# Heads paired across two groups, with 64-row by 32-column TensorE tiles for the landmark scores

## The chip, the cores and the metric

The kernel runs on one core of a Trainium2 chip. The metric is the device time of one execution in microseconds (us); of several runs the median is taken. Engines are written as the profile writes them: PE is TensorE's matmuls, PEld its weight loads, DVE is VectorE, ACT is ScalarE, POOL is GpSimd, and SP issues the DMAs.

## The reference, cut to what matters

A Nyström attention over 8 batches, 8 heads, 576 tokens and a head size of 64, with 32 landmarks, is followed by a Fourier mixing over tokens and channels, a normalisation and a two-layer network of width 2048.

```python
q_lm = q.reshape(B, H, m, S // m, D).mean(axis=3)      # m = 32 landmarks of 18 tokens
k_lm = k.reshape(B, H, m, S // m, D).mean(axis=3)
A = sm(q, k_lm)          # softmax(scale * q @ k_lm^T): 576 x 32 per head
Bm = sm(q_lm, k_lm)      # 32 x 32 per head
C = sm(q_lm, k)          # 32 x 576 per head
Z = Bm^T / (|Bm|_1 * |Bm|_inf + 1e-6)
for _ in range(6):
    Z = 2 * Z - Z @ Bm @ Z
attn = A @ Z @ C @ v
x = attn, heads side by side           # 8 x 576 x 512
u = x + real(fft(fft(x, axis=1), axis=2))
un = (u - mean(u)) / sqrt(var(u) + 1e-6)
out = u + relu(un @ w_ch1) @ w_ch2
```

## The kernel before, in words

The inputs are laid out on the host. The eight heads of a batch stand in two groups of four (`GROUPS`), and each group in two pairs. q and k lie with the head size on the partitions: a pair's two heads take rows 0 to 63 and 64 to 127 of a 128-row tile. `load(b)` brings, for each group g, one tile `kf` of k (two pairs, 1152 columns) and one tile `qf` of q (1168 columns), each by one DMA of 128 rows, then v and, for batch 0, the first pieces of the weights. These tiles come from the pool `big`.

Work of a batch is written as two Python generators. `tokens(b)` sums tokens into landmarks on DVE (`lm`: columns 0 to 63 of a group are q's, 64 to 127 k's), bounds q with a sum of absolute values on ACT (`AF.Abs`, into `am`), scales and splits q and the k landmarks into two fp16 halves, and computes A: block u = 0 and u = 1 is a group each, four token tiles by two pairs by three matmuls of 64 columns; u = 2 holds the remaining 64 tokens of both groups (the rest, tile `row`). Then come softmax, the transposed copies `AT`, the sums and differences `F1`, `F2`, `Fh` over mirrored token tiles, and the cosine and sine products `CS`. `landmarks(b)` computes B and C in fp32. Because a pair shares the 128 rows, q's landmarks are first spread into `qbd`, 64 columns a pair, with the other head's rows set to zero by a mask; one matmul of a 128-row by 64-column tile then serves both heads. C goes in two column halves of 288 per group. B's softmax, the iteration for Z (`RE`, `E`), and the folded tables `Wt`, `Wx` and `WC` follow; `mix` puts it together per token tile, `norm` normalises and hands tiles `unT` to the network.

`mlp` is the network: a chunk of 256 tokens takes 192 matmuls `h<-unT,w` (256 columns) and 96 matmuls `acc<-w,h` (512 columns). `weights` decodes the 32 weight pieces from 64-bit words at the start (PE sums their squares into `acc<-w`; from these `scale` makes the scales `wsc`) and halves them into fp16 pairs. The network's second layer can begin only when the second scale, computed from all 32 pieces, is there.

PE's order is written by the program: `run` steps the threads attention, weights and mlp by a clock of its own (`now`), and each thread says with `till` how long it would wait. While nothing is ready and the first accumulator is not yet needed, it puts matmuls `acc<-idle` on PE. The other engines' orders come from a scheduler, except for instructions that `keep_in_program_order` fixes. Every engine runs its list in order. The PSUM banks `at` of the attention are four, used in turn (`psum`); a fifth request waits until the first is read.

All calls on DVE, ACT and POOL go through `Timed.emit`, so the profile shows them at L127; all matmuls show at L210, transposes on PE at L215. In the profile's names `w` is the weights, `at` a bank of the attention, `ones` a matrix of ones.

Of the kernel before, what the change touches and what calls it, by code (L numbers as in the profile page):

```python
# [41 lines left out]
OFF = 768  # L42

# [61 lines left out]
class Timed:  # L105


    def __init__(self, kernel, engine, fixed, rate, fast):
        self.kernel, self.engine, self.fixed, self.rate, self.fast, self.free = kernel, engine, fixed, rate, fast, 0.0

    def __getattr__(self, name):
        call = getattr(self.engine, name)

        def emit(out, *args, **kw):
# [12 lines left out]
            return call(out, *args, **kw)  # L127
# [4 lines left out]
class Kernel:  # L132
    def __init__(self, ctx, tc, NB, q, k, v, w1, w2, t1, t1t, t2, diag, mask, out):
# [9 lines left out]
        self.V, self.A = Timed(self, nc.vector, 0.07, 1.04e-3, 0.52e-3), Timed(self, nc.scalar, 0.2, 0.83e-3, 0.83e-3)  # L143
# [216 lines left out]
    def load(self, b):  # L360
# [4 lines left out]
        for g in range(2):  # L365
            kf, qf = self.big(), self.big()
            gs = slice(2 * g, 2 * g + 2)
            nc.sync.dma_start(kf[:, 0 : 2 * S].rearrange("p (r t) -> p r t", r=2), self.k[b, :, gs])
            nc.sync.dma_start(qf[:, 0 : 16 * SEG].rearrange("p (r t) -> p r t", r=2), self.q[b, :, gs])
# [12 lines left out]
    def tokens(self, b, st):  # L382
# [6 lines left out]
        lm = sm.tile([P, 2, 128], F32, name="lm", bufs=1)  # L389
        am = self.small(4, "amax")  # L390
        qbd = sm.tile([P, 4, 64], F32, name="qbd", bufs=1)
        qhs = []
        for g in range(2):
            kf, qf = loads[g][0][:, 0 : 2 * S], loads[g][1][:, 0:NQ]
            first = V.tensor_reduce(lm[:, g, 64:128], kf.rearrange("p (m t) -> p m t", t=18), AX.X, ALU.add)
# [3 lines left out]
            lv = lm[:, g, 0:64].rearrange("p (x o m) -> p x o m", o=2, m=8)  # L399
# [6 lines left out]
            A.activation(qhs[g][:, 0:NQ], qf, AF.Abs, accum_out=am[:, g : g + 1])  # L406
# [18 lines left out]
        klm = sm.tile([P, 2, 2, 64], F16, name="klm", bufs=1)
        kbd = sm.tile([P, 2, 2, 2, 64], F16, name="kbd", bufs=1)
        for g in range(2):
            split(klm[:, g, 0], klm[:, g, 1], lm[:, g, 64:128], sc[:, g : g + 1])
        for h2 in range(2):
            ms, cols = self.mask2[:, h2 : h2 + 1], slice(32 * h2, 32 * h2 + 32)  # L430
            V.tensor_scalar(
                kbd[..., cols].rearrange("p g y r m -> p (g y r) m"), klm.rearrange("p g y (r m) -> p (g y r) m", r=2),
                ms, None, ALU.mult,
            )
        qm = [h[:, 0:2048].rearrange("p (y r t) -> p y r t", y=2, r=2) for h in qhs]
        qr = [h[:, 2048:2304].rearrange("p (y r t) -> p y r t", y=2, r=2) for h in qhs]
        for g in range(2):
# [6 lines left out]
            if g == 0:  # L444
                yield self.till(qhs[0], kbd)
# [90 lines left out]
    def landmarks(self, b, st):  # L536
# [39 lines left out]
        while b == 1 and self.seconds < NF // 2 - HB:  # L576
            yield 0.5
# [446 lines left out]
```

## Time and profile before

| | |
|---|---|
| median of 3 runs | 1018.75 us (1017.17 to 1018.84) |
| profiled execution | 1018.43 us, of which the profiled span is 1016.6 us |
| PE, busy share of the span | 969.0 us, 95% |
| PEld | 673.3 us, 66% |
| DVE | 608.2 us, 60% |
| ACT | 335.5 us, 33% |
| POOL | 125.9 us, 12% |
| mean granted TensorE clock | 0.98 |

How to read what follows. A row of the view by groups gives line, engine, operation, `out<-in` by the program's names, shapes and count; then busy time in us and the mean length of one in ns; then the engine's idle time before such instructions and what ended it. `128*64` is the part of the array that a matmul takes: 128 rows, 64 columns. An fp32 matmul of the program shows as two records. Matmuls are pipelined, so the length of a record is not its price; the price is the distance to the next start. A row of the timeline gives start, length, engine, operation and count, and in brackets the idle time before it with the releaser. A row of the table by stretches gives, after the stretch's bounds and length, the busy us of PE, PEld, DVE, ACT and POOL with their counts, the granted clock, the DMA share and GB/s.

### The profile page before, as it was taken

How to read it: one execution, taken by the hardware profiler on the slowest of the kernel's cores; microseconds unless marked ns; L12 is line 12 of the kernel's file. 1: busy time of each engine (PE TensorE's matmuls, PEld its weight loads, DVE VectorE, ACT ScalarE, POOL GpSimd, SP SyncE). 2: the span in 40 equal slices, each digit the busy share in tenths (PEclk: the TensorE clock that was granted, in tenths of full speed). 3: DMA queues.
4: the chain of work that ended last, by engine and by line, in shares of the span. 5: the costliest groups of instructions: out<-in, count | busy, mean ns of one | idle time of the engine just before them, and what ended most of it. 6: DMA issues, size and time to landing. Idle time of an engine off the chain costs nothing.

```text
span 1016.6 us, 20320 instructions
## 1 busy us (share of the span) xinstructions
PE 969.0 (95%) x8407; PEld 673.3 (66%) x8407; DVE 608.2 (60%) x1654; ACT 335.5 (33%) x723; POOL 125.9 (12%) x144
## 2 busy tenths in 40 slices
PE   5776989999999999999999999999999999999998
PEld 3654756667776676666766776667676676666665
DVE  6979797786655855287556855686453834351111
ACT  4658653343223322142233323332212322111110
POOL 0000000013011400024011401122020220110000
PEclk8887999999999999999999999999999999999999
DMA  9863204142312240112402240225020200120000
GB/s 328 254 250 111 83 2 167 22 71 51 148 21 45 43 164 11 43 36 53 161 12 53 50 168 6 58 48 180 1 53 11 58 15 22 22 53 21 1 22 21
DMA packets 97772, 74.63 MB, mean 73 GB/s; under 512 B 68112, under 2 KB 86544, under 8 KB 97552
## 3 DMA queue, kind: packets, MB, share of 16 engines
q1 hardware_dynamic: 97680, 73.34, 24.7%
q8 instruction: 66, 1.08, 0.5%
q14 instruction: 26, 0.21, 0.1%
HBM read 48.02 MB, written 9.44 MB: 57 GB/s over the span
## 4 chain that ended last, share of the span: by engine, by line
PE 82%; DVE 11%; ACT 3%; DMA 2%; issue 1%; POOL 1%; SPq 0%; DVEq 0%; POOLq 0%; ACTq 0%
PE h L210 34%; PE acc L210 34%; PE at L210 13%; DVE w L127 2%; DVE mid L127 1%; ACT mid L127 1%; DMA mid<-mid 1%; DVE lm L127 1%; DVE cmx L127 1%; DVE asum L127 1%; DMA big<-q_dram 1%; DMA big<-k_dram 1%; POOL mid L127 1%; PE at L215 1%; DVE amx L127 0%
## 5 line engine op out<-in xcount | busy, mean ns | idle before, releaser
L210 PE MATMUL h<-unT,w 128*128 128x256 f16 x3456 | 411.2, 273 | 0.0
L210 PEld LDWEIGHTS <-w 128*128 128x128 f16 (+1 forms) x3584 | 346.2, 99 | 73.2 <-issue 3.3
L210 PE MATMUL acc<-w,h 128*128 128x512 f16 x1680 | 394.3, 380 | 0.0
L210 PEld LDWEIGHTS <-h 128*128 128x128 f16 x1680 | 161.8, 98 | 161.9 <-issue 4.4
L127 DVE SCALAR_TENSOR_TENSOR h<-h 128x512 f16<-128x512 f32 x140 | 96.1, 687 | 198.7 <-ACT h L127 198.0
L127 ACT ACTIVATE h<-h 128x512 f16<-128x512 f32 x140 | 83.2, 595 | 308.0 <-PE h L210 295.8
L127 POOL TENSOR_TENSOR r<-ve,mhalf 128x2 f32<-128x2 f32 (+1 forms) x20 | 13.7, 685 | 411.1 <-DVE ve L127 404.1
L127 POOL TENSOR_TENSOR mid<-mid 128x640 f16<-128x640 f32 (+2 forms) x36 | 40.9, 1144 | 114.2 <-ACT mid L127 107.9
L127 DVE TENSOR_TENSOR mid<-mid 128x256 f32<-128x256 f32 (+2 forms) x68 | 45.3, 682 | 13.2 <-DMA mid<-mid 9.4
L127 DVE TENSOR_REDUCE lm<-big 128x32 f32<-128x576 f32 (+1 forms) x48 | 44.2, 946 | 10.2 <-DMA big<-k_dram 9.5
L127 DVE SCALAR_TENSOR_TENSOR u<-at,scw,row 128x128 f32<-128x128 f32 (+3 forms) x120 | 38.6, 389 | 13.8 <-PE at L210 11.8
L210 PEld LDWEIGHTS <-big 128*128 128x128 f16 (+1 forms) x768 | 39.7, 101 | 10.2 <-issue 2.8
L210 PEld LDWEIGHTS <-mid 64*128 64x128 f16 (+1 forms) x624 | 30.0, 96 | 18.8 <-issue 8.6
L127 ACT CAST row<-row 128x512 f16<-128x512 f32 (+1 forms) x40 | 20.7, 551 | 62.7 <-DVE row L127 62.7
L127 DVE SCALAR_TENSOR_TENSOR row<-at,scw,row 128x262 f32<-128x262 f32 (+1 forms) x48 | 21.3, 486 | 28.3 <-ACT row L127 21.4
L127 POOL TENSOR_TENSOR row<-row 128x512 f16<-128x512 f32 (+1 forms) x33 | 34.3, 1055 | 30.7 <-ACT row L127 28.8
L210 PE MATMUL at<-RE,E 128*128 128x96 f32 (+1 forms) x192 | 30.5, 281 | 4.3 <-DVE RE L127 4.3
L127 DVE SCALAR_TENSOR_TENSOR u<-acc,wsc,u 128x512 f32<-128x512 f32 x36 | 26.8, 749 | 12.5 <-PE acc L210 11.8
L210 PEld LDWEIGHTS at<-RE,E 128*128 128x128 f32 x192 | 27.1, 194 | 10.6 <-DVE RE L127 4.4
L210 PE MATMUL at<-mid,big 128*128 128x262 f16 (+1 forms) x288 | 31.8, 279 | 0.0
L127 DVE SCALAR_TENSOR_TENSOR big<-big,aq_r 128x1024 f16<-128x1024 f32 (+1 forms) x32 | 26.8, 868 | 3.9 <-ACT big L127 3.9
L127 ACT CAST mid<-mid 128x512 f16<-128x512 f32 (+1 forms) x28 | 18.1, 671 | 28.2 <-POOL mid L127 20.5
(166 smaller groups left out, 928.6 us busy)
## 6 DMA issues: line engine op xcount, KB each, us to landing
w<-w_dram SPq DMA_DIRECT2D x22, 512.0 KB, 8.7
big<-v_dram SPq DMA_DIRECT2D x16, 640.0 KB, 8.9
big<-q_dram SPq DMA_DIRECT2D x16, 584.0 KB, 6.0
big<-k_dram SPq DMA_DIRECT2D x16, 576.0 KB, 5.0
out_dram<-u SPq DMA_DIRECT2D x36, 256.0 KB, 2.0
big<-w_dram SPq DMA_DIRECT2D x10, 512.0 KB, 6.8
t<-t_dram SPq DMA_DIRECT2D x1, 1048.0 KB, 9.2
unT<-row SPq DMA_TRANSPOSE x64, 2.5
```

The lines of the kernel that those rows point to most:

```text
L127: return call(out, *args, **kw)
L210: self.nc.tensor.matmul(out, a, b, start=start, stop=stop, skip_group_check=True)
L215: self.nc.tensor.transpose(out, a, ident)
```

## The change

A 128-row tile now pairs a head of group 0 (rows 0 to 63) with a head of group 1 (rows 64 to 127); the loop variable e goes over the pairs within a group. Each tile of q and k is loaded by two DMAs of 64 rows.

- B and C need no `qbd`: a matmul takes 64 rows (one head) and 32 columns. A batch has 8 of them for B and 16 for C instead of 4 and 8. All four banks are asked for at once (`till(lm, banks=4)`); B's result lies in columns 288 to 319 of the first two. The two row halves write different banks.
- In A the `kbd` mask goes over the groups. Blocks u = 0 and 1 are now two token tiles each with all heads; the count of 64-column matmuls stays 48. The rest takes 24 matmuls of 32 columns instead of 12 of 64.
- One scale for q and one for k instead of one a group: `am` has two columns, `qsum` adds them, `km` is the maximum over both tiles; `scr` and its copies go. q's bound no longer waits for the landmarks.
- `F1` is formed from both A blocks, 512 columns an operation; `CS` and `mix` index accordingly.
- ACT's first ten instructions keep the program's order (`PIN`): q's two sums of absolute values come first.

```diff
+PIN = 10
...
+            ins = call(out, *args, **kw)
+            if self.pinned > 0:
+                self.kernel.tc.keep_in_program_order(ins)
+                self.pinned -= 1
+            return ins
...
-            nc.sync.dma_start(kf[:, 0 : 2 * S].rearrange("p (r t) -> p r t", r=2), self.k[b, :, gs])
-            nc.sync.dma_start(qf[:, 0 : 16 * SEG].rearrange("p (r t) -> p r t", r=2), self.q[b, :, gs])
+            for t, src, n in ((kf, self.k, S), (qf, self.q, 8 * SEG)):
+                for half in range(2):
+                    nc.sync.dma_start(
+                        t[64 * half : 64 * half + 64, 0 : 2 * n].rearrange("p (o t) -> p o t", o=2),
+                        src[b, :, 2 * half + g].rearrange("(o p) t -> p o t", o=2),
+                    )
...
-            for h2 in range(2):
-                ms, cols = self.mask2[:, h2 : h2 + 1], slice(32 * h2, 32 * h2 + 32)
-                V.tensor_scalar(
-                    qbd[:, 2 * g : 2 * g + 2, cols], lm[:, g, 0:64].rearrange("p (r m) -> p r m", r=2), ms, None, ALU.mult
-                )
-            yield self.till(qbd)
+            yield self.till(lm)
...
+        V.tensor_tensor(qs, am[:, 0:1], am[:, 1:2], ALU.add)
+        eq, rq = self.power(qs, 1, 2.0**-13, "aq", b == 1)
...
+            if u < 2:
+                pt = ps.rearrange("p (j g r m) -> p j g r m", j=2, g=2, r=4)
+                for j in range(2):
+                    for r in range(4):
+                        at = 128 * (2 * u + j)
+                        mm3(pt[:, j, :, r], lambda y: qm[r // 2][:, y, r % 2, at : at + 128], lambda y: kbd[:, y, r // 2, r % 2].rearrange("p (g m) -> p g m", g=2))
+            else:
+                for r in range(4):
+                    for g in range(2):
+                        mm3(ps[64 * g : 64 * g + 64, 32 * r : 32 * r + 32], lambda y: qr[r // 2][:, y, r % 2],
+                            lambda y: kbd[:, y, r // 2, r % 2, 32 * g : 32 * g + 32])
...
-        ps = self.psum()
-        for g in range(2):
-            for pr in range(2):
-                mm(ps[64 * pr : 64 * pr + 64, 32 * g : 32 * g + 32], qbd[:, 2 * g + pr], lm[:, g, 64 + 32 * pr : 96 + 32 * pr])
-        V.tensor_scalar(Bd.rearrange("p g m -> p (g m)"), ps[:, 0:64], 1.0 / 2592.0, None, ALU.mult)
+        while b == 1 and self.seconds < NF // 2 - HB:
+            yield 0.5
+        yield self.till(lm, banks=4)
+        heads = [(slice(64 * g, 64 * g + 64), slice(32 * r, 32 * r + 32), g, r // 2, r % 2) for r in range(4) for g in range(2)]
+        halves = [[self.psum() for g in range(2)] for hf in range(2)]
+        for half, row, g, e, o in heads:
+            mm(halves[0][g][row, 288:320], lm[half, 0, e, 32 * o : 32 * o + 32], lm[half, 1, e, 32 * o : 32 * o + 32], share=0.3)
+        for hf in range(2):
+            for half, row, g, e, o in heads:
+                kv = loads[e][0][half, S * o + 288 * hf : S * o + 288 * hf + 288]
+                mm(halves[hf][g][row, 0:288], lm[half, 0, e, 32 * o : 32 * o + 32], kv, share=0.21)
```

Three places show how the lists of the engines move. The first is ACT at the program's start; `big,amax<-big` are q's sums of absolute values, `mid,csum<-at,cb` C's exponentials, `row<-w` and `w<-w` the decoding of weights. Before:

```order
L127 ACT_TABLE_LOAD
L127 ACTIVATE row<-w_74 128x512
L127 ACTIVATE Bd<-Bd 128x64
L127 ACTIVATE row<-w_74 128x512
L127 ACTIVATE w_73<-w_74 128x512
L127 ACTIVATE mid,csum<-at,cb 128x288 x3
L127 ACTIVATE big,amax<-big 128x1168 x2
L127 ACTIVATE mid,csum<-at,cb 128x288
```

And now:

```order
L130 ACT_TABLE_LOAD
L130 ACTIVATE big,amax<-big 128x1168 x2
L130 ACTIVATE row<-w_74 128x512
L130 ACTIVATE Bd<-Bd 128x64
L130 ACTIVATE mid,csum<-at,cb 128x288 x4
L130 ACTIVATE row<-w_74 128x512
L130 ACTIVATE w_73<-w_74 128x512
L130 ACTIVATE klm<-lm,sc 128x128
```

The two sums stand ahead of everything else and no longer behind three exponentials; weight decoding moves back.

The second is DVE ahead of batch 0's first normalised tile (`unT`), on which the network's first matmul waits; `w_73<-w_73,wsc` halves a piece of the first layer. Before:

```order
L127 SCALAR_TENSOR_TENSOR r_992<-rt,r_990 128x2
L127 SCALAR_TENSOR_TENSOR w_73<-w_73,wsc 128x512
L127 TENSOR_SCALAR row<-u,mv,r_992 128x512 x2
L127 SCALAR_TENSOR_TENSOR w_73<-w_73,wsc 128x512
L127 SCALAR_TENSOR_TENSOR w_74<-row,w_74 128x512
L127 SCALAR_TENSOR_TENSOR w_73<-w_73,wsc 128x512
L127 SCALAR_TENSOR_TENSOR unT<-at,unT 128x4x128 x2
```

And now:

```order
L130 SCALAR_TENSOR_TENSOR r_986<-rt,r_984 128x2
L130 SCALAR_TENSOR_TENSOR w_73<-w_73,wsc 128x512
L130 TENSOR_SCALAR row<-u,mv,r_986 128x512 x2
L130 SCALAR_TENSOR_TENSOR w_73<-w_73,wsc 128x512
L130 SCALAR_TENSOR_TENSOR w_74<-row,w_74 128x512 x2
L130 SCALAR_TENSOR_TENSOR unT<-at,unT 128x4x128
```

Over the whole list, 10 halvings and 23 decodings stood ahead of the first `unT`; now 3 and 20 do.

The third is DVE between the second scale (`wsc`) and the landmarks of batch 1, which PE waits for; `big<-big,aq_r` splits q, `lm<-big` are the landmark sums. Before:

```order
L127 TENSOR_SCALAR wsc<-wp_e 128x1
L127 SCALAR_TENSOR_TENSOR w_74<-w_74,wsc 128x512
L127 SCALAR_TENSOR_TENSOR h<-h 128x512
L127 SCALAR_TENSOR_TENSOR w_74<-w_74,wsc 128x512 x3
L127 SCALAR_TENSOR_TENSOR h<-h 128x512
L127 SCALAR_TENSOR_TENSOR w_74<-w_74,wsc 128x512 x4
L127 TENSOR_REDUCE lm<-big 128x64
```

And now:

```order
L130 TENSOR_SCALAR wsc<-wp_e 128x1
L130 SCALAR_TENSOR_TENSOR big<-big,aq_r 128x1024
L130 SCALAR_TENSOR_TENSOR h<-h 128x512
L130 SCALAR_TENSOR_TENSOR w_74<-w_74,wsc 128x512
L130 SCALAR_TENSOR_TENSOR big<-big,aq_r 128x128
L130 SCALAR_TENSOR_TENSOR w_74<-w_74,wsc 128x512
L130 SCALAR_TENSOR_TENSOR big<-big,aq_r 128x1024
```

The four operations that split q moved ahead of the landmark sums; before, they stood behind C.

More of the change, by code (lines that the diff above doesn't have):

```diff
@@ L388, in tokens @@
         NQ = 16 * SEG
-        lm = sm.tile([P, 2, 128], F32, name="lm", bufs=1)
-        am = self.small(4, "amax")
-        qbd = sm.tile([P, 4, 64], F32, name="qbd", bufs=1)
+        lm = sm.tile([P, 2, 2, 64], F32, name="lm", bufs=1)
+        am = self.small(2, "amax")
         qhs = []
-        for g in range(2):
-            kf, qf = loads[g][0][:, 0 : 2 * S], loads[g][1][:, 0:NQ]
-            first = V.tensor_reduce(lm[:, g, 64:128], kf.rearrange("p (m t) -> p m t", t=18), AX.X, ALU.add)
+        for e in range(2):
+            kf, qf = loads[e][0][:, 0 : 2 * S], loads[e][1][:, 0:NQ]
+            first = V.tensor_reduce(lm[:, 1, e], kf.rearrange("p (m t) -> p m t", t=18), AX.X, ALU.add)
             if b == 1:
                 self.tc.keep_in_program_order(first)
-            lv = lm[:, g, 0:64].rearrange("p (x o m) -> p x o m", o=2, m=8)
+            lv = lm[:, 0, e].rearrange("p (x o m) -> p x o m", o=2, m=8)
             qv = qf.rearrange("p (x o t) -> p x o t", o=2, t=2 * SEG)
@@ L414, in tokens @@
-        st["loads"], st["qbd"], st["lm"] = loads, qbd, lm
+            A.activation(qhs[e][:, 0:NQ], qf, AF.Abs, accum_out=am[:, e : e + 1])
+            yield self.till(lm)
+        kb = self.small(2, "kb", BF16)
+        km, qs = self.small(1, "kmax"), self.small(1, "qsum")
+        V.tensor_reduce(km, lm[:, 1].rearrange("p e m -> p (e m)"), AX.X, ALU.max, apply_absolute_value=True)
+        st["loads"], st["lm"] = loads, lm
         self.spawn(self.landmarks(b, st))
-        eq, rq = self.power(am[:, 0:2], 2, 2.0**-13, "aq", b == 1)
@@ L425, in tokens @@
+        sc = self.small(2, "sc")
+        V.tensor_tensor(sc[:, 0:1], eq, rk, ALU.mult)
+        V.tensor_scalar(sc[:, 1:2], ek, 1.0 / 144.0, None, ALU.mult)
         klm = sm.tile([P, 2, 2, 64], F16, name="klm", bufs=1)
         kbd = sm.tile([P, 2, 2, 2, 64], F16, name="kbd", bufs=1)
+        split(*(klm[:, y].rearrange("p e m -> p (e m)") for y in range(2)), lm[:, 1].rearrange("p e m -> p (e m)"), sc[:, 0:1])
         for g in range(2):
-            split(klm[:, g, 0], klm[:, g, 1], lm[:, g, 64:128], sc[:, g : g + 1])
@@ L539, in landmarks @@
         V, A = self.V, self.A
-        loads, qbd, lm = st["loads"], st["qbd"], st["lm"]
+        loads, lm = st["loads"], st["lm"]
         m4g = lambda m: self.mask4.unsqueeze(1).unsqueeze(3).broadcast_to([P, 2, 4, m])
@@ L574, in landmarks @@
         V.tensor_tensor(BTd, wide(BT, 32), m4g(32), ALU.mult)
-        while b == 1 and self.seconds < NF // 2 - HB:
-            yield 0.5
         for g in range(2):
-            kv = loads[g][0][:, 0 : 2 * S].rearrange("p (r t) -> p r t", r=2)
             Ce = self.mid()
@@ L584, in landmarks @@
             csum, cmx = self.small(2, "csum"), self.small(2, "cmx")
[L585 removed]
             for hf in range(2):
[L587 to L591 removed]
+                V.tensor_reduce(cmx[:, hf : hf + 1], halves[hf][g][:, 0:288], AX.X, ALU.max)
             cb = self.small(1, "cb")
```

90 lines of the change are left out of this document (29 added, 61 removed).

## The prediction

> **What bounds the kernel.** I read the page first, then the table by stretches.
>
> ```profile
> PE 969.0 (95%) x8407; PEld 673.3 (66%) x8407; DVE 608.2 (60%) x1654; ACT 335.5 (33%) x723; POOL 125.9 (12%) x144
> ```
>
> ```profile
> 119.50:140.00 20.50, 16.40 (x90) 7.57 (x88) 19.79 (x56) 13.43 (x26) 0.00 (x0) 1.00 0.00 0
> 175.00:1016.00 841.00, 832.79 (x7106) 572.87 (x7104) 462.28 (x1253) 233.02 (x512) 117.94 (x127) 1.00 0.20 54
> ```
>
> From 175 us to the end PE is busy for 832.79 of 841 us at full clock, while DVE, ACT and POOL are idle about half the time or more. So there a microsecond of matmuls saved is a microsecond of the span, and work saved on the other engines is worth nothing. Between 119.5 and 140 us it is the reverse: DVE is busy for 19.79 of 20.5 us and PE waits. Before that come the loads, batch 0 and the decoding of the weights, a stage set by chains. I therefore make three sums: batches 2 to 7, batch 1, and the start.
>
> **Batches 2 to 7: B and C.** The timeline of PE in batch 2, and two places later and earlier where the array is shared by several small tiles:
>
> ```profile
> 218.50 0.43 PE L210 MATMUL at<-lm,qbd 128*64 128x32 f32 x8
> 218.76 2.14 PE L210 MATMUL at<-big,qbd 128*64 128x288 f32 x16
> 220.83 1.04 PE L210 MATMUL acc<-w,h 128*128 128x512 f16 x4
> ...
> 235.58 1.73 PE L210 MATMUL at<-big,mid 128*32 128x64 f32 x80
> 237.24 1.27 PE L210 MATMUL at<-kbd,big 128*128 128x64 f16 x36
> ...
> 189.69 0.84 PE L210 MATMUL at<-Wx,mid 64*128 64x128 f16 x24
> 190.46 2.14 PE L210 MATMUL h<-unT,w 128*128 128x256 f16 x18
> ```
>
> B and C take 220.83 - 218.50 = 2.33 us. C's 16 records run in pairs, one on each 64-column half: 2.07 / 8 = 0.259 us a pair. Afterwards C has 32 records on eight tiles (two row halves, four column strips). Eight at a time that is 4 x 0.259 = 1.04 us; B's 16 records are two rounds where four pairs took 0.26 us, so 0.13 us; together 1.17 us. If only four ran at a time, C would stay at 8 x 0.259 = 2.07 us and B at 0.26 us: no gain. No row shows rows and columns divided at once, but each division is shown alone. Four 32-column strips: 80 records in 1.66 us are 0.021 us each, where 64 columns at the pair's pace need 0.259 x 64/288 = 0.058 us. Two row halves: 24 records in 0.77 us are 0.032 us each, where half of an `h` record (below, 0.109 us) is 0.055 us. Both run side by side, and the halves write different banks, as the changed kernel's do. So I take a value near the good end, 1.25 us: a gain of 1.08 us a batch.
>
> **Batches 2 to 7: A.** The 48 large matmuls keep their columns and their weight loads, so they cost what they cost. The rest goes from 12 matmuls of 64 columns to 24 of 32. Batch 1 shows the blocks apart:
>
> ```profile
> 145.65 0.87 PE L210 MATMUL at<-kbd,big 128*128 128x64 f16 x24
> 146.36 0.67 PE L210 MATMUL at<-RE,E 128*128 128x96 f32 x4
> ...
> 149.48 1.26 PE L210 MATMUL at<-kbd,big 128*128 128x64 f16 x36
> 150.67 0.69 PE L210 MATMUL at<-RE,E 128*128 128x96 f32 x4
> ```
>
> A block of 24 takes 0.71 us (0.030 each); with the rest it is 1.19 us, so the rest's 12 take 0.48 us. Twice as many of half the columns cost between nothing, if columns decide, and 0.48 us more, if the count does. On two column halves side by side each half has 12 at 0.030 = 0.36 us; I take +0.13 us. Sum: 6 x (-1.08 + 0.13) = -5.7 us.
>
> [...]
>
> What else leaves or joins these batches is covered. The `qbd` and `scr` operations, one scale in place of two, and the wider `F1` lie on DVE, which has 841 - 462 us to spare; a `CS` that starts later, since `F1` needs both blocks, has network matmuls beside it, and the program's own clock places them. Four more load issues a batch stand in SP's list ahead of stores and transposes; the DMA share is 0.20.
>
> **Batch 1.** PE's timeline there, DVE's beside it, and the prices of the groups that stand in DVE's new list:
>
> ```profile
> 131.36 0.31 PE L210 MATMUL at<-lm,qbd 128*64 128x32 f32 x4
> 133.83 0.31 PE L210 MATMUL at<-lm,qbd 128*64 128x32 f32 x4 [2.16 <-DVE qbd L127]
> 133.96 2.14 PE L210 MATMUL at<-big,qbd 128*64 128x288 f32 x16
> 137.51 0.16 PE L210 MATMUL at<-kb,ones 128*128 128x2 bf16 x1 [1.40 <-ACT mid L127]
> ```
>
> ```profile
> 117.61 0.21 DVE L127 TENSOR_SCALAR wsc<-wp_e 128x1 f32<-128x1 f32 x1
> 125.89 2.67 DVE L127 TENSOR_REDUCE lm<-big 128x64 f32<-128x1152 f32 x3
> 130.12 2.67 DVE L127 TENSOR_REDUCE lm<-big 128x64 f32<-128x1152 f32 x3
> ```
>
> ```profile
> L127 DVE SCALAR_TENSOR_TENSOR w<-w,wsc 128x512 f16<-128x512 f32 x32 | 23.9, 747 | 2.1 <-ACT w L127 1.4
> L127 DVE SCALAR_TENSOR_TENSOR big<-big,aq_r 128x1024 f16<-128x1024 f32 x16 | 21.4, 1336 | 3.5 <-ACT big L127 3.5
> L127 DVE SCALAR_TENSOR_TENSOR big<-big,aq_r 128x128 f16<-128x128 f32 x16 | 6.4, 401 | 0.4 <-ACT big L127 0.4
> L127 DVE TENSOR_SCALAR Bd<-at 128x64 f32<-128x64 f32 x8 | 1.8, 221 | 4.6 <-PE at L210 4.5
> ```
>
> PE stands twice, 2.16 and 1.40 us. From the second scale (117.61) to the last landmark sum DVE needed 132.79 - 117.61 = 15.2 us. In the new list there stand two large and two small splits of q (2 x 1.336 + 2 x 0.401), nine halvings (6.7), two halves of the network's `h` (2 x 0.69) and the six sums (5.3): 16.9 us. PE comes to B after 51 `acc` matmuls in place of 54. Those took (131.36 - 119.49) / 54 = 0.22 us each, so PE is there 1.9 + 11.2 = 13.1 us after the scale and stands 3.8 us, 1.5 more than now (2.16 and the piece of B done early). Then `kb`'s matmul, directly behind C as before, needs the bank that C's first exponential frees: 137.51 - 133.96 = 3.55 us after C's start, and B is now read in two operations, 0.2 more. C ends after 1.25 us, so PE stands 2.5 us, 1.1 more. Against that C's 1.08 and the rest's 0.13: batch 1 loses 1.6 us. The bounds are 0, if the sums come no later than now, and +3.2, if C gains nothing either and the same waits stand.
>
> **The start.** DVE's wait for q's sums, two later rows of it, PE's timeline, and SP's first issues:
>
> ```profile
> 21.06 0.17 DVE L127 TENSOR_SCALAR aq_e<-amax 128x2 f32<-128x2 f32 x1 [1.49 <-ACT big L127]
> ...
> 109.71 0.68 DVE L127 SCALAR_TENSOR_TENSOR w<-row,w 128x512 int32<-128x512 int32 x1
> 114.48 0.69 DVE L127 SCALAR_TENSOR_TENSOR h<-h 128x512 f16<-128x512 f32 x1 [2.39 <-ACT h L127]
> ```
>
> ```profile
> 85.29 1.94 PE L215 MATMUL at<-ident,row 128*128 128x128 f32 x8 [5.68 <-DVE row L127]
> 91.88 4.09 PE L210 MATMUL h<-unT,w 128*128 128x256 f16 x36
> 95.81 0.39 PE L210 MATMUL acc<-w 128*128 128x128 bf16 x4
> 114.31 0.62 PE L210 MATMUL acc<-w 128*128 128x128 bf16 x8
> 119.49 10.64 PE L210 MATMUL acc<-w,mid 128*128 128x512 f16 x48
> ```
>
> ```profile
> 1.19 0.42 SPq L368 DMA_DIRECT2D big<-k_dram  x1
> 1.66 0.42 SPq L369 DMA_DIRECT2D big<-q_dram  x1
> 3.31 1.16 SPq L347 DMA_DIRECT2D w<-w_dram  x2
> ```
>
> Everything later shifts with the first `acc<-w,h` matmul, at 119.49. It needs all 32 pieces decoded and squared. The last decoding ended at 110.4, but PE came to the last squares only at 114.31, behind 150 `h` matmuls of (95.81 - 91.88) / 36 = 0.109 us, and DVE then waited 2.39 us. So the network's first matmul, 91.88, set the pace; it waits for batch 0's normalised tiles, and those for DVE (5.68 us of idle PE ahead of 85.29). In the new list DVE has 7 halvings (5.2 us) and 3 decodings (2.0 us) fewer ahead of the first `unT`: the first `h` up to 7 us earlier. PE then has 12 more `h`, four more groups of squares and 12 idle matmuls before the last squares: 1.3 us, up to 1.2 (0.62 us for eight records, and these are sixteen), and 1.3 (256 columns, as an `h`), 3.8 us more. That leaves 3.4 us. DVE's total up to the second scale hardly changes, so its decoding ends earlier only by idle time taken out: the 1.49 us in which it waits for q's sums on ACT, now first, and what the shorter C frees. I take -3.4 us. The bounds are -6, if nearly all of the 7 us stays, and +1.9: four more load issues ahead of the first weight piece, 1.66 - 1.19 = 0.47 us each (3.31 would become 5.2), if the transfers before it do not hide them; the weights start the whole chain.
>
> **Sum.** The profiled execution took 1018.43 us, 0.3 below the median of the runs. 1018.4 - 5.7 + 1.6 - 3.4 = 1010.9 us. With the bounds, the likeliest case spans 1006 to 1015.
>
> **Rivals.**
> - Slower: the banks. C now holds all four banks, and `kb`'s matmul waits for the first to be read. In batches 2 to 7 it stands 24 network matmuls behind C, about 3.9 us, so 5.1 us after C's start, while batch 1's chain needs 3.75. If DVE is late by one q tile's split (1.34 + 0.40) and a pair of `h` halves (1.4), PE stands 1.8 us in each batch: 6 x 1.8 = 10.8, and 1021.6 us. It decides from 1.3 us a batch on. Against it: PE lost only about 8 us to idling in the whole stretch after 175 us, with five bank requests around C before. Chance 0.10.
> - The change does not do what it says: tiles divided both ways run only four at a time. Then 1018.4 + 6 x 0.13 + 2.7 - 3.4 = 1018.5 us. Chance 0.08.
> - The start brings nothing, or the late weights cost 1.9 us: 1014.3 to 1016.2 us. For it: DVE's total is unchanged. Chance 0.16.
> - [...] Chance 0.05.
>
> **How the numbers follow.** The forecast has 0.61. Differences of 0.2%, 2.0 us, are about what a measurement can tell from no change. Faster by more: 0.61 + 0.05 + 0.15 of the third rival + 0.01 of the second = 0.82; within: 0.01 + 0.06 + 0.02 of the first = 0.09; slower: 0.01 + 0.08 = 0.09. The range takes in the start's and the third rival's ends and the four-wide case: 1004.5 to 1018.
>
> **What would show it.** Right: C's 32 records within about 1.15 us and B within 0.2; the rest of A under 0.65 us; the first `h` near 85 to 88 and the first `acc<-w,h` near 116; PE idle in batch 1 near 6 us; after 175 us about as little idle PE as now. Wrong: pairs of C's records 0.25 us apart without eight starts close together, `kb` or `nrm` waiting for ACT in every batch, or a second scale later than 117.6.

## The result, and the profile after

The changed kernel takes 1028.66 us (median of 4 runs, 1027.36 to 1033.35) where the kernel before takes 1018.8: a ratio of 1.0104, 95% interval 1.0074 to 1.0134. It is 10 us slower; the forecast was 7.5 us faster. The profiled execution took 1028.87 us with a span of 1027.1, against 1018.43 and 1016.6 before, so the two traces show the difference: 10.5 us of span.

The first section of the page, busy time of each engine:

```profile
PE 967.9 (94%) x8710; PEld 672.9 (66%) x8710; DVE 599.2 (58%) x1598; ACT 336.4 (33%) x715; POOL 125.8 (12%) x144
```

PE's busy time is 1.1 us less, while the span is 10.5 us longer: PE waits more. Part of the busy time is also dearer. The table by stretches (busy time of PE, PEld, DVE, ACT and POOL, then the granted clock, the DMA share and GB/s) shows both; first the changed kernel, then the kernel before for the one stretch that the prediction doesn't show:

```profile
119.50:140.00 20.50, 17.14 (x113) 9.62 (x111) 17.32 (x34) 13.13 (x21) 0.56 (x1) 1.00 0.00 1
140.00:160.00 20.00, 16.50 (x254) 10.83 (x255) 15.49 (x61) 9.00 (x22) 0.00 (x0) 0.83 0.12 31
175.00:1016.00 841.00, 830.36 (x7378) 574.38 (x7377) 460.01 (x1222) 234.94 (x510) 118.46 (x128) 1.00 0.25 56
```

```profile
140.00:160.00 20.00, 20.00 (x259) 15.26 (x258) 19.47 (x61) 9.18 (x22) 2.63 (x3) 1.00 0.01 2
```

From 140 to 160 us PE stands for 3.5 us and runs at 0.83 of its clock. After 175 us it stands for 10.6 of 841 us, before for 8.2 (half of that before batch 2's B).

**Where it was lost.** Since both kernels issue the same network matmuls, a place in one trace can be set against the same place in the other: I take the start of each batch's B, and correct it for the `h` and `acc` matmuls that are done by then (0.109 and 0.216 us each, the median distance of their starts). The difference between two such places is the lag that was gained or lost between them. The last three columns are worked out in the same way for all kernels of this document: PE's idle time in batches 2 to 7, and the time lost to a clock below full in batch 1 and in batches 2 to 7 (slices of 4 us, 1 minus the granted clock).

```
                       lag against before, us          PE idle  clock lost     profiled  median
kernel                 at batch 1  batch 1  2 to 7     2 to 7   b. 1  2 to 7   us        us
before                     0          0       0          4.1    1.7   0        1018.43   1018.75
after (as changed)        +7.7       +2.2    +0.6       10.0    3.4   0        1028.87   1028.66
e1  whole loads           +2.8       +1.8    +7.1       11.2    3.4   5.1      1030.02   1029.28
e2  table load early      +5.6       +1.9    -0.2        9.1    3.4   0        1025.59   1025.83
e3  old + its loads       +5.1       -2.7    -0.5        3.8    0     0        1020.27   1019.42
e4  e1 + norm. on DVE     +1.9       +4.5    -2.6        6.2    6.8   0        1022.25   1022.15
e5  e4 + kb's own bank    +1.1       -1.5    -2.2        6.5    3.4   0        1016.09   1017.38
e6  e1 - pin              +0.3       +1.9    +6.4       10.5    3.4   5.1      1027.20   1021.56
e7  e1 + F1 by block      +0.7       -0.2    +1.3        7.0    1.7   3.4      1020.23   1020.96
e8  old + norm. on DVE    +0.7       -2.9    +0.8        4.4    0     0        1017.16   1017.83
e9  e5 - pin              -1.6       -4.0    -2.8        5.9    0     0        1010.13   1012.54
e10 e5 + F1 by block      +1.1       -4.3    -3.5        5.7    0     0        1011.86   1013.24
e11 e5 with split loads   +7.3       -3.4    -4.2        5.2    0     0        1018.28   1018.80
e12 e10 - pin             -0.2       -2.9    -3.2        6.0    1.7   0        1012.25   1012.95
e13 after + kb's bank     +6.7       -2.6    +0.6        9.9    0     0        1023.17   1023.76
e14 after + norm. on DVE  +6.4       +1.7    -3.3        6.0    3.4   0        1023.25   1026.16
e15 old + pin             -2.7       +1.3    -0.6        3.7    3.4   0        1016.47   1015.87
```

So the change lost 7.7 us in the start, 2.2 in batch 1 and 0.6 in batches 2 to 7, where the prediction had -3.4, +1.6 and -5.7.

A lag is read from one execution, so it scatters. Up to batch 1's B, e1, e4 and e5 execute the same instructions in the same order on PE, DVE and ACT, and their lags there are 2.8, 1.9 and 1.1 us; so do the changed kernel, e11, e13 and e14, with 7.7, 7.3, 6.7 and 6.4. Two lags at batch 1 that differ by less than about 1.7 us show no difference. The clock columns leave out the start, where half the clock cost 18.8 us before and 23.9 in the changed kernel; how much of the 7.7 us that is was not separated.

**B and C did what was forecast.** PE's timeline in batch 2, as shown of before:

```profile
221.85 0.27 PE L217 MATMUL at<-lm 64*32 64x32 f32 x13
...
221.96 1.16 PE L217 MATMUL at<-big,lm 64*32 64x288 f32 x29
223.05 2.12 PE L217 MATMUL acc<-w,h 128*128 128x512 f16 x9
```

223.05 - 221.85 = 1.20 us in place of 2.33. Eight tiles run side by side: within a round of C the eight starts lie about 7 ns apart, and the rounds follow each other every 0.243 us.

**Batches 2 to 7: new waits took it back.** The waits of PE and, in the second fence, of DVE from 175 to 1016 us (in total, times, longest):

```profile
PE at L217 <- DVE RE L130: 7.5, 7, 2.2
PE at L217 <- DVE u L130: 1.6, 2, 0.8
PE acc L217 <- DVE u L130: 0.9, 1, 0.9
```

```profile
DVE mid L130 <- POOL mid L130: 8.5, 5, 2.2
```

Before, they were:

```profile
PE at L210 <- DVE RE L127: 2.0, 2, 1.6
```

```profile
DVE mid L127 <- POOL mid L127: 2.6, 3, 0.9
```

PE idles 5.9 us more in these batches (10.0 against 4.1), against about 5.3 us less matmul work. DVE's timeline in batch 3, and what PE does there:

```profile
357.82 0.31 DVE L130 TENSOR_SCALAR RE<-at,cr,ci 128x64 f32<-128x64 f32 x1
360.09 0.87 DVE L130 TENSOR_TENSOR mid<-mid 128x512 f32<-128x512 f32 x1 [1.96 <-POOL mid L130]
360.88 0.33 DVE L130 TENSOR_SCALAR RE<-at,cr,ci 128x64 f32<-128x64 f32 x1
361.14 1.95 DVE L130 TENSOR_TENSOR mid<-mid 128x512 f32<-128x512 f32 x2
```

```profile
361.27 0.46 PE L217 MATMUL at<-RE,E 128*128 128x96 f32 x2 [1.00 <-DVE RE L130]
```

The `mid<-mid` of 512 columns is the first half of `F1`, which now needs both blocks of A. It stands in DVE's queue for 1.96 us until POOL has normalised the second block, and the small `RE` for the other group, of the chain for which PE waits, stands behind it.

**Batch 1.** PE's timeline:

```profile
126.69 3.67 PE L217 MATMUL acc<-w,mid 128*128 128x512 f16 x15 [1.06 <-DVE w L130]
130.73 7.07 PE L217 MATMUL acc<-w,mid 128*128 128x512 f16 x32 [0.37 <-DVE w L130]
...
140.05 0.23 PE L217 MATMUL at<-lm 64*32 64x32 f32 x4 [1.41 <-DVE lm L130]
...
140.14 1.15 PE L217 MATMUL at<-big,lm 64*32 64x288 f32 x28
144.60 0.16 PE L217 MATMUL at<-kb,ones 128*128 128x1 bf16 x1 [3.31 <-ACT mid L130]
144.63 4.00 PE L217 MATMUL acc<-w,h 128*128 128x512 f16 x9
```

The two waits ahead of B are for halvings of weights (`w`), which on DVE now stand behind the splits of q. `kb`'s one column waits 3.31 us for a bank, and behind it nine `acc` matmuls take 4.00 us, twice what they take elsewhere (2.12 above): the clock is halved for about 7 us, which costs 3.4.

**The start.** SP's first issues and ScalarE's first instructions, of the changed kernel:

```profile
1.19 1.38 SPq L376 DMA_DIRECT2D big<-k_dram  x2
...
6.50 1.14 SPq L354 DMA_DIRECT2D w<-w_dram  x2
```

```profile
9.04 1.28 ACT L130 ACT_TABLE_LOAD   x1 [9.04 <-DMA big<-q_dram]
10.34 1.18 ACT L130 ACTIVATE big<-big 128x1168 f16<-128x1168 f32 x1
...
14.19 1.18 ACT L130 ACTIVATE big<-big 128x1168 f16<-128x1168 f32 x1 [2.58 <-DMA big<-q_dram]
```

The first piece of the weights is issued at 6.50 us (before 3.31). ScalarE's table load, at 0.73 us before, now waits for q: the first pinned instruction waits for two DMAs, and one of the two waits stands at the table load (9.04 us of idle ScalarE, ended by `big<-q_dram`). The first `h` comes at 89.85 (before 91.88), as forecast somewhat earlier, but DVE ends the last decoding at 116.45 (before 110.39), the last squares start at 120.95 (114.71) and the first `acc<-w,mid` at 125.25 (119.49).

### The profile page after: what moved, and what is told of

It is laid out like the page before. It is cut to its first block, busy times and chain, and to the rows that moved or that the text cites. A ratio compares the mean times of both kernels' runs of the same rounds, so it can differ in the third digit from the quotient of the medians.

```text
span 1027.1 us, 20948 instructions
## 1 busy us (share of the span) xinstructions
PE 967.9 (94%) x8710; PEld 672.9 (66%) x8710; DVE 599.2 (58%) x1598; ACT 336.4 (33%) x715; POOL 125.8 (12%) x144
## 4 chain that ended last, share of the span: by engine, by line
PE 75%; DVE 10%; DMA 5%; issue 4%; ACT 2%; POOL 2%; SPq 1%; POOLq 0%; DVEq 0%; ACTq 0%
PE h L217 32%; PE acc L217 31%; PE at L217 12%; DVE mid L130 2%; DMA w<-w_dram 2%; DVE w L130 2%; POOL mid L130 1%; DMA mid<-mid 1%; DVE u L130 1%; DMA diag<-ny_dram 1%; DVE asum L130 1%; DVE h L130 1%; PE at L222 1%; ACT mid L130 1%; DVE lm L130 1%
## 5 line engine op out<-in xcount | busy, mean ns | idle before, releaser
L130 DVE TENSOR_TENSOR mid<-mid 128x256 f32<-128x256 f32 (+3 forms) x52 | 39.7, 794 | 17.8 <-DMA mid<-mid 8.7
L130 DVE SCALAR_TENSOR_TENSOR row<-at,scw,row 128x262 f32<-128x262 f32 (+1 forms) x48 | 21.4, 486 | 29.5 <-ACT row L130 20.9
L217 PE MATMUL acc<-idle,ones 128*128 128x256 bf16 x140 | 26.9, 338 | 1.5 <-DVE idle L175 1.5
```

The lines of the kernel that those rows point to most:

```text
L130: ins = call(out, *args, **kw)
L217: self.nc.tensor.matmul(out, a, b, start=start, stop=stop, skip_group_check=True)
```

## The experiments

### The loads (e1, e3, e16, e17) and the table load (e2)

e1 undoes the loads:

```
-                for half in range(2):
-                    nc.sync.dma_start(
-                        t[64 * half : 64 * half + 64, 0 : 2 * n].rearrange("p (o t) -> p o t", o=2),
-                        src[b, :, 2 * half + g].rearrange("(o p) t -> p o t", o=2),
-                    )
+                nc.sync.dma_start(t[:, 0 : 2 * n], src[b, :, g])
...
-    ... .reshape(NB, 4, 2 * D, S).transpose(0, 2, 1, 3)          (k; q likewise)
+    ... .reshape(NB, 2, 2, 2, D, S).transpose(0, 1, 4, 2, 3, 5).reshape(NB, P, 2, 2 * S)
```

> The changed kernel with k and q stored on the host so that each tile is again loaded by one DMA of 128 rows with 4608 or 4672 contiguous bytes a row (the change loads each tile by two DMAs of 64 rows with two pieces of 2304 or 2336 bytes a row). Everything else as changed; as its first sum then waits for one load only, ScalarE's table load waits for none. Theory L (the loads cost the start): the lag of 7.7 us at batch 1's B falls to between 0 and +3, the first weight issue is back near 3.3 us, and the time is 1019 to 1023 us. Theory O (the new order of DVE's and ScalarE's work in the start costs it, the loads are hidden): less than 2 us of it goes, 1026.5 us or more. The waits after 175 us (about 10 us) stay under both.

Measured: 1029.28 us, ratio 1.0102 (1.0081 to 1.0122), no faster. The step that theory L spoke of came as it said (weights issued at 3.24 us, lag at batch 1 from 7.7 to 2.8), its time did not. The table shows why: batches 2 to 7 lost 7.1 us in place of 0.6, 5.1 of it to three stretches at half the clock which the changed kernel's trace doesn't have, 1.2 to more idle time. One of them follows two waits for `RE` (1.09 and 0.50 us); the changed kernel has the same two waits in the same place (1.04 and 0.50 us). The difference lies in where the waits fall. In every trace here all changes of the granted clock lie on a grid of 3.41 us (the stretches at half the clock last 3.41, 6.83 or 13.65 us before, and 3.41, 6.83, 13.65 or 17.07 in the changed kernel), so I cut the traces into windows of that grid. First e1: its two waits, the window that holds both, and the next one; then the same of the changed kernel, where the waits fall into two windows.

```profile
481.58 0.46 PE L217 MATMUL at<-RE,E 128*128 128x96 f32 x2 [1.09 <-DVE RE L130]
482.55 0.46 PE L217 MATMUL at<-RE,E 128*128 128x96 f32 x2 [0.50 <-DVE RE L130]
```

```profile
479.68:483.09 3.41, 1.82 (x10) 0.92 (x9) 2.66 (x5) 1.30 (x3) 2.62 (x4) 1.00 0.48 96
483.09:486.50 3.41, 3.41 (x16) 2.05 (x15) 1.95 (x5) 1.26 (x3) 2.94 (x4) 0.50 0.56 53
```

```profile
484.35 0.46 PE L217 MATMUL at<-RE,E 128*128 128x96 f32 x2 [1.04 <-DVE RE L130]
485.31 0.46 PE L217 MATMUL at<-RE,E 128*128 128x96 f32 x2 [0.50 <-DVE RE L130]
```

```profile
481.54:484.96 3.42, 2.23 (x11) 0.89 (x8) 1.77 (x4) 1.30 (x3) 3.05 (x4) 1.00 0.38 77
484.96:488.37 3.41, 3.06 (x25) 2.50 (x26) 2.56 (x6) 1.10 (x3) 2.52 (x5) 1.00 0.73 81
```

In e1 both waits lie in one window, PE is busy for 1.82 of its 3.41 us (53%), and the next window runs at half the clock. In the changed kernel they are spread over two windows, busy for 2.23 and 3.06 us (65% and 90%), and the clock stays full. Over all nineteen traces, a window at full clock with PE busy for less than 43% of it was followed by half the clock each time (64 of 64), one with more than 56% never (none of 5192), and between these shares 28 of 54 were; in the traces of before and of the changed kernel alone it was 7 of 7, none of 547 and 6 of 12. So the same waits can halve the clock in one execution and not in another, and a comparison of two kernels that both have such waits can hide or invent 2 to 5 us (one halved window is 1.7 us, e1's three are 5.1); the table's columns separate the two.

e3 does the loads alone, in the kernel before:

```
-            nc.sync.dma_start(kf[:, 0 : 2 * S]..., self.k[b, :, gs])
+            for half in range(2):
+                rows = slice(64 * half, 64 * half + 64)
+                nc.sync.dma_start(t[rows, 0 : 2 * w]..., src[b, gs, rows].rearrange("r p t -> p r t"))
```

> The kernel before, with the change's loads alone: each tile by two DMAs of 64 rows with two pieces of 2304 or 2336 bytes a row. Theory L: the first weight issue moves from 3.3 to about 6.5 us, decoding and the first acc<-w,h matmul move by 4 to 7 us, and the time is 1023 to 1026 us. Theory O: the loads are hidden, 1018 to 1020.5 us.

Measured: 1019.42 us, ratio 1.0008 (0.9998 to 1.0018). Again the step came (first `h`, last squares and first `acc` all 5.1 us later) and the time did not: batch 1 gave 2.7 us back, 1.7 of it a clock that stays full there and 0.9 less idle time of PE (5.7 us against 6.6). DVE's and ACT's lists moved with the loads, from 16.9 and 20.9 us on, so e3 changes more than the loads' pace.

What about these loads is slow, e16 and e17 tell: the pieces alone (one DMA of 128 rows, two pieces a row) and the rows alone (two DMAs of 64 rows, one piece a row), both in the kernel before.

> The kernel before, each k and q tile loaded by one DMA of 128 rows, but in two pieces of 2304 or 2336 bytes a row. Theory S (small pieces halve what the queue moves): about 190 GB/s over the first 14 us, as in e3 and in the changed kernel, where the kernel before moved 293. [...]

> The kernel before, each k and q tile loaded by two DMAs of 64 rows, each row in one piece of 4608 or 4672 bytes. Theory S: 270 GB/s or more over the first 14 us. [...]

The first 14 us by stretches, DMA share and GB/s last: before, the changed kernel, e16, e17.

```profile
0.00:14.00 14.00, 8.80 (x57) 6.25 (x59) 8.76 (x21) 1.94 (x2) 2.06 (x8) 0.97 0.88 293
```

```profile
0.00:14.00 14.00, 7.42 (x47) 5.26 (x47) 5.33 (x10) 2.55 (x3) 2.07 (x8) 1.00 0.84 188
```

```profile
0.00:14.00 14.00, 8.76 (x57) 6.24 (x59) 8.70 (x21) 1.95 (x2) 2.06 (x8) 0.95 0.88 294
```

```profile
0.00:14.00 14.00, 7.40 (x45) 5.45 (x45) 5.75 (x12) 1.28 (x1) 2.06 (x8) 0.98 0.84 191
```

It is the 64 rows that slow the transfers. The DMA engines are nearly as busy (0.84 against 0.88) and move two thirds (191 GB/s in e17 against 293 before); pieces of half the size cost no rate (294 in e16). What each costs in time these runs do not tell: it is one execution each, 1020.22 and 1019.14 us beside 1019.38 of the kernel before, with lags at batch 1 of 2.4 and 2.3 us where e3 had 5.1.

e2 leaves the loads and puts a tiny operation first on ScalarE:

```
+        first = nc.scalar.activation(self.cp.tile([P, 2], F32, name="warm"), self.mhalf, AF.Abs)
+        tc.keep_in_program_order(first)
```

> The changed kernel with one tiny ScalarE operation (128x2, Abs of a constant) pinned ahead of q's two sums, so that ScalarE's table load doesn't stand behind the landing of q's first half. Loads stay as changed. Theory L: the sums start at most 1.3 us earlier and q's second half lands no sooner, so the time is the same within 1.5 us, 1027 to 1030. Theory T (the table load behind q sets the start): q's first sum moves from 10.3 to about 9.1 us, and the lag of 7.7 us falls by 2 us or more: 1026 us or less.

Measured: 1025.83 us, ratio 1.0062 (1.0038 to 1.0086). The table load is back at 0.73 us, q's first sum at 8.96, and although q's second half lands as late as before (14.03), the lag at batch 1 falls by 2.1 us, the least that theory T asked for, and all four runs (1023.63 to 1026.21 us) lie below the changed kernel's. The lag of 5.6 us is 0.8 to 2.1 less than those of the four kernels with the changed kernel's start (6.4 to 7.7). So of the 4.9 us between the changed kernel and e1 one or two belong to the table load's wait, which the halved loads brought with them: with one DMA a tile the first sum has one wait, and the table load none (in e15, with the same pin and one DMA a tile, it starts at 0.73 us).

### Batches 2 to 7: DVE behind POOL (e4, e7, e8, e14)

e4 takes the wait away by letting DVE normalise; e14 is the same edit in the changed kernel itself, e8 in the kernel before:

```
-            (self.G if b > 0 else V).tensor_tensor(av, av, bc(asum), ALU.mult)
+            V.tensor_tensor(av, av, bc(asum), ALU.mult)
```

> As e1 (whole loads), and the normalisation of the two large blocks of A (mid<-mid,asum 128x512) goes from POOL to DVE in all batches, so that DVE's F1 never stands in its queue waiting for POOL. Theory Q (in batches 2 to 7 DVE's in-order queue, stopped by F1 that waits for POOL's normalisation, makes RE late and PE wait): PE's waits for DVE's RE after 175 us fall from 7.5 us to about 2, and it is 4 to 6 us faster than e1. Rival D (DVE is simply late with its work; two more operations of 0.7 us on it change nothing or make it worse): within 1.5 us of e1 or slower.

> The changed kernel with one edit: the normalisation of A's two large blocks on DVE. Theory Q: PE's waits for RE after 175 us fall from 7.5 to about 3.5 us: 1023 to 1025.5 us, so that e13 and e14 share e11's 10 us about evenly. Theory K (kb's bank in batch 1 is nearly all of it): 1027 us or more.

> The kernel before, with the normalisation of A's two large blocks on DVE instead of POOL. Theory Q (the blocking came with the change): before, PE waited for RE 2.0 us in all, so there is little to win: 1017 to 1019.5 us. Rival (POOL's normalisation was a cost of this kernel all along): 3 us or more faster than before, so that e4's gain is none of the change's.

e4: 1022.15 us, 7.1 less than e1, and e14: 1026.16, ratio 1.0064 (1.0042 to 1.0087). Not all of e4's gain is DVE's: batches 2 to 7 gave 9.7 us, about half of it idle time of PE (11.2 to 6.2) and half the clock (5.1 to 0), and batch 1 lost 2.7. e8: 1017.83, ratio 0.9996 (0.9985 to 1.0008): nothing to win in the kernel before, so the stop came with the change. In e14 batches 2 to 7 go from +0.6 to -3.3 us, since PE idles 6.0 us instead of 10.0; its waits for `RE` fall to 4.0 us (3.5 expected; in e4 to 4.6, where about 2 were expected). Its median moved by 2.5 us only, between what theories Q and K said, and its interval overlaps the changed kernel's. Its seven runs go with their clock: three with a mean granted clock of 0.973 to 0.977 took 1020.4 to 1023.5 us, the profiled one among them, and four with 0.966 to 0.969 took 1026.2 to 1028.9.

e7 leaves POOL its work and forms `F1` within a block, `F2` between them:

```
-        F1 = [self.mid()[:, 0:512] for _ in range(2)]
-        for x, op in enumerate((ALU.add, ALU.subtract)):
-            V.tensor_tensor(F1[x], aes[0], aes[1], op)
+            if u < 2:
+                F1.append(self.mid()[:, 0:512])
+                for x, op in enumerate((ALU.add, ALU.subtract)):
+                    V.tensor_tensor(F1[u][:, 256 * x : 256 * x + 256], ae[:, 0:256], ae[:, 256:512], op)
...
```

> As e1 (whole loads), with F1 formed block by block (sum and difference of the two 256-column halves of one block, as the kernel before did), and F2 between the two blocks; the same number of DVE and POOL operations, normalisation on POOL as changed. Theory Q1 (it is the wider F1, which needs both normalised blocks at once, that stops DVE's queue): PE's waits for RE fall as in e4, from 7.5 us to 3 or less, and it is 4 to 7 us faster than e1. Rival Q2 (any F1 behind POOL's normalisation stops DVE, wide or not; the two blocks now share one exponential scale and finish together): waits as in e1 within 2 us, and 0 to 2 us faster.

Measured: 1020.96 us, ratio 1.0017 (1.0006 to 1.0028), 8.3 less than e1. DVE's waits for POOL and PE's for `RE`, of e7:

```profile
DVE mid L130 <- POOL mid L130: 2.0, 4, 0.6
```

```profile
PE at L217 <- DVE RE L130: 5.4, 6, 1.4
```

DVE's stop falls from 8.5 to 2.0 us with the same work on the same engines. (`F1` is four operations of 256 columns a batch instead of two of 512, so DVE has 16 operations more in all, not the same number.) That `F1` needs both blocks at once was the cause of the stop. PE's waits for `RE` fall less than theory Q1 said (7.9 to 5.4); the rest of the gain is lag in the start (2.8 to 0.7, of which most can be scatter) and clock (3.4 us less lost).

### Batch 1: kb's bank (e5, e13)

```
+        own = self.ps_h.tile([P, 512], F32, name="h") if b == 1 else None
-        ek, rk = self.bound(kb, 1, 2.0**-13, "ak")
+        ek, rk = self.bound(kb, 1, 2.0**-13, "ak", own)
```

> As e4 (whole loads, normalisation on DVE), and in batch 1 kb's one-column matmul takes a bank of the network's h pool, so that it doesn't wait for the first of C's four banks to be read. Theory K (the bank is what PE stands for): the wait of 3.61 us ahead of kb goes to under 1 us and with it the halved clock behind it (3.4 us in the 4-us slices from 136 to 148 us); 3 to 6 us faster than e4, 1016 to 1019 us. Rival (what stands behind kb on PE needs the same chain, so the wait only moves to the next matmul): within 1.5 us of e4.

> The changed kernel with one edit: kb's matmul of batch 1 takes a bank of the network's h pool. Theory K: the 3.31 us ahead of kb and the halved clock behind it (3.4 us) go, most of it as time: 1022 to 1025 us. Theory Q (only DVE's stop behind POOL counts, in batches 2 to 7): 1026.5 us or more.

e5: 1017.38 us, 4.8 less than e4. `kb` in e5, where it waited 3.61 us in e4:

```profile
133.79 0.16 PE L217 MATMUL h<-kb,ones 128*128 128x1 bf16 x1 [0.35 <-DVE kb L130]
```

e13, this edit alone in the changed kernel: 1023.76 us, ratio 1.0044 (1.0027 to 1.0061), 4.9 less, within theory K's numbers; batch 1 goes from +2.2 to -2.6 us. The idle time in batch 1 falls by 2.0 us only (7.8 to 5.8, since the next waits, for `nrm` and the transposes, stay): the larger part, 3.4 us, is the clock that is no longer halved. Both edits in the changed kernel are e11 (below, 1018.8 us): of its 10 us they win back 9.9.

### The pin, and what adds up (e6, e9 to e12, e15)

e6 is e1 and e9 is e5 with `PIN = 0`; e15 is the kernel before with the pin alone (`PIN = 10` and the lines that use it); e11 is e5 with the changed kernel's loads; e10 is e5 with `F1` as in e7, and e12 is e10 with `PIN = 0`.

> As e1 (whole loads), without the pin of ScalarE's first ten instructions, so that the pairing of heads stands alone. Theory N (the pin costs nothing once the table load is free): within 1.5 us of e1, 1028 to 1031, lag at batch 1's B 2 to 4 us. Theory P (the pin itself delays the decoding of the weights): 2 us or more faster than e1, lag under 1 us. Theory G (the pin is a gain of the order of the 3 us by which kb's first matmul came earlier): 2 us or more slower.

> As e5 (whole loads, normalisation on DVE, kb with a bank of its own), without the pin of ScalarE's first ten instructions. Theory P (the pin delays the decoding of the weights by the 2.5 us that the lag at batch 1's B differed between e1 and e6): lag there 1.1 falls below 0, 1.5 to 3 us faster than e5, 1014.5 to 1016 us. Theory N (the pin costs nothing, and the 7.7 us between e1 and e6 were mostly stretches of halved clock that fell otherwise): within 1.5 us of e5.

> The kernel before, with ScalarE's first ten instructions pinned to the program's order, and nothing else. Theory P (the pin delays the decoding by 2 to 3 us whatever the heads): 1020.5 to 1022.5 us, last squares 2 us or more later than 114.7. Theory N (only together with the paired heads, whose B and C come as one piece, does it cost): 1018 to 1019.5 us.

Measured: e6 1021.56 us, ratio 1.0028 (1.0015 to 1.0042); e9 1012.54, ratio 0.9948 (0.9929 to 0.9966), the lowest median of all and below what either theory said; e15 1015.87, ratio 0.9964 (0.9949 to 0.9978). With the paired heads the pin costs 2.5 and 2.7 us of lag at batch 1 (e1 to e6, e5 to e9), and 1.3 from e10 to e12; the larger differences in time have clock in them. In e9 the stretches of half the clock in batch 1 are gone. Of e6's ten runs the profiled one was the slowest (1027.20 us, mean clock 0.973); the other nine took 1019.2 to 1024.0 at 0.976 to 0.980, where e1's four had 0.970 to 0.973. In the kernel before, the same pin is a gain of 3.6 us, which neither theory foresaw. The first 60 us by stretches tell the two apart, DVE's busy time third and ACT's fourth; e5, e9 and e15:

```profile
0.00:60.00 60.00, 41.26 (x475) 31.77 (x476) 47.62 (x146) 33.30 (x72) 2.06 (x8) 0.83 0.83 282
```

```profile
0.00:60.00 60.00, 40.78 (x504) 31.67 (x505) 51.42 (x155) 36.35 (x80) 2.06 (x8) 0.89 0.89 301
```

```profile
0.00:60.00 60.00, 41.29 (x431) 31.64 (x431) 50.29 (x154) 34.38 (x72) 2.07 (x8) 0.86 0.88 299
```

DVE does 3.8 us more by 60 us without the pin in the paired kernel, and e15 2.2 us more than the kernel before (48.10). In e5 the second piece's magnitude on ScalarE starts at 17.10 us, behind q's sums and the four exponentials, in e9 at 12.76, ahead of them; DVE's decoding waits for it. In e15 the work that stands ahead of q's sums is itself a decoding (13.05 us), so that less is put off. That the order of these first rows is the whole cause was not tried.

> As e5, with F1 formed block by block as in e7. Theory Q1 (F1's width matters by itself, also where DVE normalises): PE's waits for RE after 175 us fall from 4.8 us to 3 or less, 1 to 3 us faster than e5. Theory Q3 (e7 and e4 removed the same stop of DVE's queue behind POOL; once it is gone the form of F1 is worth nothing): within 1.2 us of e5.

> As e5, with the change's loads (two DMAs of 64 rows a tile, and so ScalarE's table load behind q's first half again). It is the changed kernel with the normalisation on DVE and kb's bank alone. Theory L (loads and table load cost the start 5 us, which e1's time didn't show since the clock halved three times more later): lag at batch 1's B 5 to 7.7 us, 1021 to 1024 us. Theory O (that lag is given back later, as in e3, where 5.1 us of lag ended as 1.0 us of time): 1017 to 1019 us.

> All four mends together: whole loads, normalisation on DVE, kb's bank, F1 by block, and no pin. If the parts add (no pin 4.8 us from e5 to e9, F1 by block 4.1 from e5 to e10, medians): 1008 to 1010 us. If both only took away the same halved clock in batch 1 and the same RE waits (theory S, shared): 1011.5 to 1014, as e9 and e10.

e10: 1013.24 us, ratio 0.9950 (0.9935 to 0.9966), 4.1 less than e5: more than either theory said, but 2.8 us of lag went in batch 1, where e5 lost 3.4 us to a low clock and e10 none; batches 2 to 7 gained 1.3, as Q1 said. e11: 1018.80 us, ratio 1.0001 (0.9988 to 1.0014): the lag at batch 1 is 7.3 us, as theory L said, and yet only 1.4 us of time more than e5, theory O's number. e12: 1012.95 us, ratio 0.9944 (0.9931 to 0.9957): the mends don't add. Without the pin nothing is won on e10 but 1.3 us of lag, and that is lost to the clock.

## Why the prediction was wrong

- **B, C and A, batches 2 to 7: right.** C and B took 1.20 us (1.25 forecast), so -1.13 a batch. A's rest takes 0.49 us a batch, from its first start to the next matmul's where no wait stands between, against 0.40 before, so +0.10 (+0.13 forecast). 6 x (-1.13 + 0.10) = -6.2, a little better than the forecast; the table gives about -5.3 (0.6 less 5.9 of idle time). The four-wide rival fell: eight starts lay 7 ns apart in C. The 0.05 among the chances stands for a least distance between the starts of matmuls, which no run shows: beside the 7 ns in C, the rest's 24 lay on average 16.5 ns apart.
- **"What else leaves or joins these batches is covered": the step that failed there.** It counted DVE's free time (841 - 462 us) for the wider `F1`. DVE's work was not too much; it stood in order. The wider `F1`, with a later input than its neighbours, held up what was behind it (for 1.96 us in batch 3), on an engine that is idle 45% of that stretch. The term at nothing measured +5.9 us of PE's idle time; e14 takes 3.9 us of the stage's time back, and e7 shows that it is `F1`.
- **Batch 1: +1.6 forecast, +2.2 measured, by other terms.** The wait for the sums was 1.41 us, not 3.8, in good part because PE itself came later, 14.5 us after the scale in place of 13.1: ahead of B it had waited 1.06 and 0.37 us for halvings (`w`) that now stand behind the splits of q; `kb` waited 3.31 us, not 2.5, since a halving, B's first operations and all four maxima of C stand on DVE ahead of the first exponential (140.77 to 143.86 us); and the halved clock, 3.4 us where before lost 1.7, was in no term.
- **The start: -3.4 forecast, +7.7 of lag measured; the largest miss by the lag.** At the first `acc<-w,mid`, where the forecast was made, it is +5.8; 1.4 more are PE's two waits for halvings behind it. The step that failed is "So the network's first matmul, 91.88, set the pace". The bound of +1.9 took four more issues at the 0.47 us of a whole load. An issue of 64 rows holds SP for 0.63 to 0.69 us (two in 1.26 to 1.38), and the transfers move 188 GB/s in place of 293, so the loads were not a matter of issues alone. Whole loads take 4.9 us of lag off (e1), the table load's part in it one or two (e2), the pin 1.3 to 2.7 (e6, e9, e12). The idea that an early first `h` is a gain fell too: in e1 the first `h` is 7 us earlier (84.83), the upper end of the forecast, and the last squares 1.0 us later (115.72). The decoding sets them: they start 4.3 us behind its end before, 4.5 in the changed kernel and in e1, whose last decoding ends at 111.22.
  Not all of this lag became time. The loads cost 5.1 us of lag in the kernel before and about 1 us of time, not clear of none (e3), and 6.2 us of lag and 1.4 us of time between e5 and e11; the batches behind gave the rest back. The time itself came back with the two edits in batch 1 and on DVE: e11 takes 1018.80 us with a lag of 7.3.
  The rate itself, which was in no term, goes by the rows: e17 moved 191 GB/s with 64 rows, e16 294 with 128.
- **The pin** was counted as the 1.49 us by which q's sums come earlier. Alone it is a gain, of 2.7 us of lag (e15); beside the paired heads it is a loss, and the second piece of the weights starts later on ACT. That this delay is the cause is argued, not shown.
- **The rival of the banks** had the right place, `kb` behind C's four banks, but in the wrong batches: after 175 us `kb` never waits.

The sum was -7.5 us; it came to +10.5. The chance of 0.09 for slower rested on one mechanism in batches 2 to 7, while of the three that took place two (order on DVE, clock) stood at nothing and the third (rows of the load) only as a bound of +1.9 for its issues.

## What to carry to other kernels

- When an operation is widened to take two producers' outputs, look not at its engine's free time but at what stands behind it in that engine's order, and who waits for that.
- Keep transfers over all 128 rows, and arrange the data outside for it: the same bytes in 64 rows moved at two thirds of the rate (191 against 294 GB/s, e17 and e16). Where the first loads start a long chain, that was several microseconds of lag here (5.1 in e3, 6.2 between e5 and e11), of which 1.4 us or less ended as time.
- Price a wait of PE by what the clock does behind it as well: here PE idle for about half of a window of 3.41 us or more could cost 1.7 us on top (e1: busy for 53% of a window, the next at 0.50). Before believing a small difference between two kernels set their granted clock side by side.

## What the runs showed of the hardware that was not expected

- All changes of the granted clock lie on a grid of 3.41 us in each of the nineteen traces, and after a window at full clock the next one went by how much of it PE was busy: below 43% it ran at half the clock (64 of 64), above 56% at full clock (all 5192), and between them at either (28 of 54 at half). So `kb`'s wait of 3.31 us, which left PE busy for 1.08 us of a window (140.21 to 143.62 us), was followed by two windows at 0.50, which cost as much again (3.4 us), while waits of 1.09 and 0.50 us cost 1.7 us only where both fell into one window. What decides between 43% and 56% stays open.
- Two waits on ScalarE's first operation put one of them at the table load ahead of it: 1.28 us of loading that a kernel with one wait has done by 2.0 us began at 9.04.
- Eight tiles of 64 rows and 32 columns run at once in float32: 1.20 us for 24 matmuls of the program (48 records), where pairs on two column halves took 2.33 us for the 12 (24 records) that did the same work.
